# Seven half-block products for eight in the last transform chunks of layer two, fuller score steps, and an earlier gate for one layer norm

## The chip, the cores and the metric

One Trainium2 chip, one of its cores. The metric is the device time of one launch in microseconds; lower is better. The profile is one execution, recorded instruction by instruction.

## The reference

Two layers, each an attention block with a compressive memory and then a Fourier block, on 2048 rows of 512, with 32 heads of 16 in 4 segments of 512 rows:

```python
qs, ks, vs = q[:, :, s], k[:, :, s], v[:, :, s]
logits = einsum("bhqd,bhkd->bhqk", qs, ks) * scale + mask
a_dot = einsum("bhqk,bhkd->bhqd", softmax(logits), vs)
a_mem = einsum(phi(qs), M) / (einsum(phi(qs), z) + 1e-6)
o = g * a_mem + (1.0 - g) * a_dot
M, z = M + einsum(phi(ks), vs), z + phi(ks).sum
...
a = einsum("bsd,ed->bse", x, dft_hid_re)
b = einsum("bsd,ed->bse", x, dft_hid_im)
y = einsum("ts,bse->bte", dft_seq_re, a) - einsum("ts,bse->bte", dft_seq_im, b)
...
x = x + A(layernorm(x)); x = x + B(layernorm(x))
x = x + A(layernorm(x)); x = x + B(layernorm(x))
```

The second transform, along the sequence, is the largest product: 2048 x 2048 cosines on `a` and as many sines on `b`, in each layer.

## The kernel before

Products are made from pairs of half-precision numbers, a high and a low part, so that each takes three matmuls (`mm3`: high by high, high by low, low by high).

The program's order is not written by hand. Each part is a generator (`s_x`, `s_st`, `s_f` and so on) that yields what its next step needs: an engine, tiles to read, buffers to take, or a gate, a condition on what was done. The class `Plan` keeps a model of each engine's clock, of tiles and of buffers (52 of work in SBUF, 8 banks of PSUM), and the loop at the end of `body` always issues the step that could begin first by that model. So the instructions of an engine stand in a fixed order that follows from the planner's costs, and at run time each engine takes its own in that order. `ready` adds a reserve to some reads. All recorded instructions have the line of the helper that issues them (L249 before), so the profile names them by tiles: `w` is a work buffer, `b` a PSUM bank, `g` the transposed norm of a segment, `qst` and `kst` the queries and keys of a group, `vt` its values, `mx` the maxima of its scores, `mhl` their negatives in two halves, `y` the sum of the Fourier block (and at the start a place for raw weights), `cs` the raw table of cosines and sines, `cc` its prepared copy in DRAM, `fyu` the scale that a piece of it was divided by.

**Attention** goes by segment (`q`, 8 in two layers) and group of 8 heads (4 a segment; `i` counts all 32). `s_ln` loads a segment's four row tiles, `t_ln` norms them and writes them transposed into `xt`. It begins a segment `q` when the values of the last group of the segment before are projected, `gate(("V", q * NG - 1))`. `s_p` and `s_v` project. `s_x` makes the scores once for their row maxima (`t_max` on DVE), `s_st` makes them again transposed with the maxima folded in; `t_sel` takes the exponential on ACT and zeroes what lies above the diagonal on POOL; `s_av` multiplies by the values. A step of `s_x` or `s_st` fills two PSUM banks, one for each half of the heads (64 rows of the array each, side by side). For key tile `t` of four a score block is 128, 256, 384 or 512 columns wide, and a step holds as many blocks of one `t` as fit into 512: 11 steps a group, four of them with 384 columns.

**The Fourier block.** `s_ab` makes `a` and `b` of a row tile (the matmuls with `wd`), `t_ab` splits them into `ab`. `s_r` loads the raw tables once, `s_c` finds a scale for each batch of four pieces and splits and stores them. `s_f` then multiplies: a chunk is two row tiles, eight chunks a layer; for each of 16 output tiles `t` the unit (chunk `j`, `t`) is 12 matmuls of 512 columns (2 row tiles, 2 for `a` and `b`, 3 for the parts), which DVE scales and adds into `y`:

```python
for i, (x, z) in enumerate(((0, 0), (0, 1), (1, 0))):
    T.matmul(p, c[:, x, sl], b[:, z], start=(k == 0 and i == 0), stop=(k == 4 * n - 1 and i == 2))
...
spawn(t_y(p, layer, t, fyu[:, f:f + 1]), hots)
```

Layer two's units stand in the order of chunks; each output tile is stored after its eighth unit. Layer one keeps this form in the change too.

## Time and profile before

| | |
|---|---|
| median of 3 runs | 1781.19 us (1776.84 to 1781.40) |
| the profiled execution | 1784.39 us, span 1782.6 us |
| mean granted clock | 0.975 |
| matmuls, loads of weights | 11020 each |
| DMA | 242.43 MB, mean 136 GB/s |

The span runs from the first to the last instruction. A row of the profile gives a group of instructions: line, engine, operation, output and inputs, partitions x columns and type, count, then busy time in us and the mean length of one in ns, then the idle time of the engine just ahead of them and what ended it. The lengths of matmuls overlap, so what one takes in a stream is its group's busy time, or the distance of starts, divided by the count. PEld is the loading of weights, SPq the queue of SP, which issues all DMAs in order.

### The profile page before, as it was taken

The numbers are of one execution on the slowest core, as the hardware profiler recorded it, in microseconds if no ns is written. First come the engines' busy times: TensorE is split into PE (matmuls) and PEld (weight loads), VectorE is DVE, ScalarE is ACT, GpSimd is POOL, SyncE is SP. The second block draws the span as 40 slices with busy tenths as digits, with TensorE's granted clock in tenths as the row PEclk, the third lists the DMA queues.
The fourth block names the chain that finished last, engine by engine and source line by source line (L and its number), as shares of the span: only waits on it lengthen the run. The fifth ranks groups of instructions, "written<-read, shape, count | busy, mean of one in ns | idle before, by whom it ended". The sixth has DMA issues, their size and how long they took to land.

```text
span 1782.6 us, 32540 instructions
## 1 busy us (share of the span) xinstructions
PE 1676.7 (94%) x11020; PEld 733.9 (41%) x11020; DVE 1086.1 (61%) x3387; ACT 911.4 (51%) x1585; POOL 755.4 (42%) x1187
## 2 busy tenths in 40 slices
PE   4978799999999999999899998999999999999999
PEld 2424334344444433444444443444444443344444
DVE  7783777477667775545577656754676566342222
ACT  4567666756656758433456764556355535510000
POOL 6354545546544655433335543433553343330000
PEclk9978899999999999999899999999999999999999
DMA  8446536555555533435856745453453542137104
GB/s 214 118 129 155 163 106 142 174 154 154 150 134 158 164 90 116 133 123 171 237 160 195 206 138 131 100 138 110 118 126 107 164 99 71 51 107 254 42 0 136
DMA packets 240983, 242.43 MB, mean 136 GB/s; under 512 B 129776, under 2 KB 152304, under 8 KB 240816
## 3 DMA queue, kind: packets, MB, share of 16 engines
q1 hardware_dynamic: 240816, 240.35, 48.5%
q8 instruction: 87, 1.43, 0.4%
q14 instruction: 80, 0.66, 0.1%
HBM read 152.96 MB, written 63.70 MB: 122 GB/s over the span
## 4 chain that ended last, share of the span: by engine, by line
PE 67%; DMA 11%; DVE 7%; ACT 5%; POOL 4%; issue 4%; SPq 2%; POOLq 0%; ACTq 0%; DVEq 0%
PE b L249 67%; ACT w L249 5%; POOL w L249 3%; DMA w<-w 3%; DVE w L249 2%; SPq L249 2%; DVE junk L249 2%; DMA dc<-den 2%; DMA w<-rec 2%; DMA w<-in_cs_dram 1%; DVE cam L249 1%; DVE bst L249 1%; DMA w<-in_x_dram 1%; DVE y L249 0%; DMA d<-w 0%
## 5 line engine op out<-in xcount | busy, mean ns | idle before, releaser
L249 PE MATMUL b<-w,w 128*128 128x512 f16 x3072 | 714.1, 382 | 12.5 <-ACT w L249 7.1
L249 PEld LDWEIGHTS <-w 128*128 128x128 f16 x4992 | 465.4, 99 | 624.4 <-issue 111.2
L249 POOL TENSOR_TENSOR w<-w,w 128x512 f16<-128x512 f32 (+1 forms) x316 | 379.6, 1208 | 369.1 <-ACT w L249 255.3
L249 ACT ACTIVATE w<-b,fac 128x512 f32<-128x512 f32 (+1 forms) x728 | 420.0, 657 | 205.6 <-PE b L249 196.2
L249 DVE CUSTOM_DVE_ANT_0 junk<-b,cmask 128x128 bf16<-128x128 f32 (+3 forms) x1024 | 441.1, 484 | 105.3 <-PE b L249 104.2
L249 POOL TENSOR_SCALAR_AFFINE_SELECT w<-w 128x128 f32<-128x128 f32 (+2 forms) x704 | 242.8, 356 | 308.6 <-ACT w L249 285.2
L249 DVE SCALAR_TENSOR_TENSOR y<-b,fyu,y 128x512 f32<-128x512 f32 x232 | 173.3, 747 | 220.4 <-PE b L249 219.7
L249 ACT ACTIVATE w<-b 128x512 f16<-128x512 f32 (+1 forms) x240 | 137.9, 597 | 178.7 <-PE b L249 172.3
L249 ACT ACTIVATE w<-w,csc 128x512 f16<-128x512 f32 (+1 forms) x256 | 181.9, 723 | 70.2 <-DVE csc L249 53.6
L249 PE MATMUL b<-g,w 128*128 128x512 f16 x768 | 187.5, 386 | 3.6 <-DMA g<-w 2.8
L249 PE MATMUL b<-wd,w 128*128 128x512 f16 x768 | 181.4, 382 | 0.1
L249 ACT ACTIVATE w<-w 128x512 f16<-128x512 f32 (+1 forms) x144 | 90.5, 631 | 177.9 <-DVE w L249 122.1
L249 PE MATMUL b<-w,vt 128*32 128x512 f32 (+3 forms) x2048 | 177.7, 455 | 1.9 <-POOL w L249 1.7
L249 DVE SCALAR_TENSOR_TENSOR w<-b,w 128x512 f16<-128x512 f32 x128 | 87.8, 687 | 100.4 <-ACT w L249 100.0
L249 PE MATMUL b<-kst,qst 62*128 62x128 f16 (+3 forms) x1024 | 124.7, 305 | 18.1 <-ACT w L249 5.6
L249 PE MATMUL b<-qst,kst 64*128 64x512 f16 (+3 forms) x1024 | 121.1, 304 | 13.3 <-ACT w L249 7.7
L249 PE MATMUL b<-w,g 128*128 128x128 f16 x1536 | 97.4, 221 | 11.9 <-DMA w<-w 6.9
L249 PEld LDWEIGHTS <-g 128*128 128x128 f16 x1536 | 89.7, 99 | 26.9 <-issue 17.7
L249 PEld LDWEIGHTS b<-w,vt 128*32 128x32 f32 x2048 | 56.5, 111 | 96.4 <-issue 51.1
L249 PE MATMUL b<-wo,w 128*128 128x512 f16 x384 | 88.0, 385 | 0.9 <-ACT w L249 0.9
L249 PEld LDWEIGHTS <-kst 64*128 64x128 f16 x1024 | 37.5, 94 | 124.5 <-issue 118.8
L249 DVE TENSOR_REDUCE cam<-w 128x1 f32<-128x512 f32 x128 | 81.0, 675 | 6.8 <-DMA w<-in_cs_dram 6.7
(101 smaller groups left out, 902.8 us busy)
## 6 DMA issues: line engine op xcount, KB each, us to landing
w<-in_cs_dram SPq DMA_DIRECT2D x128, 256.0 KB
cc<-w SPq DMA_DIRECT2D x128, 256.0 KB
w<-cc SPq DMA_DIRECT2D x128, 256.0 KB
w<-w SPq DMA_DIRECT2D x96, 256.0 KB
d<-w SPq DMA_DIRECT2D x128, 128.0 KB
w<-rec SPq DMA_DIRECT2D x56, 256.0 KB
w<-in_x_dram SPq DMA_DIRECT2D x32, 256.0 KB
qst<-d SPq DMA_DIRECT2D x64, 128.0 KB
```

What stands on the lines that cost most here:

```text
L249: r = f(*args, **kw)
```

## The change

**Seven products for eight.** In layer two, chunks five to seven (`WIN` = 5) no longer go through units. For a chunk and a pair of output tiles `t`, `t+1` the tables form a block matrix of two by two (a block: 128 outputs by 256 of the chunk's inputs), and the chunk's `a`, `b` another one of two by two (halves of 256 columns). The product of the two, eight block products before, is made by seven products of sums and differences (`t_win`, six matmuls of 256 columns each, in three PSUM banks), which DVE adds into `y` in halves. Four blocks of the tables are combined ahead of time from the raw ones (`s_b`: DVE or POOL adds, ACT and DVE split, SP stores them as `sc`), from the end of layer two's first segment on. The combinations of `a` and `b` are made in `t_six`, after `t_full` has taken them from PSUM at full precision. The two tiles of a pair share one scale, so `s_c` takes the maximum over both. Per pair four tiles of tables are loaded for two before (`win`), the last as a half. The last chunk's output tiles are stored two at a time (`t_out`).

**Fuller score steps.** `steps` lets a step hold blocks of different `t`: in `s_x` those of 128 with those of 384 columns, in `s_st` the same for the second and fourth key tile. 10 steps a group, all of 512 columns. `s_av` takes the key tiles in the order 0, 2, 1, 3.

**The gate of segment two.** `s_ln` begins segment two (`q` = 1) when the first group's value products are done (`("E", 0)`), no longer when the last group's values are projected.

**The planner's reserve** in `ready` is 1500 ns (`AGAIN`) where the first entry of what is read's key is `"y"`; `key` gives a pair of the tile's full name and a row for tiles kept by rows, as `y` is.

```diff
+WIN = 5
...
+AGAIN = 1500.0
...
-            r = max(r, self.wr.get(n, 0.0) + (RESERVE.get(self.by.get(n), 0.0) if eng == "T" else 500.0 * (eng != "Y" and self.by.get(n) == "Y")))
+            r = max(r, self.wr.get(n, 0.0) + (AGAIN if n[0] == "y" else RESERVE.get(self.by.get(n), 0.0) if eng == "T" else 500.0 * (eng != "Y" and self.by.get(n) == "Y")))
...
-                yield gate(("V", q * NG - 1))
+                yield gate(("E", 0) if q == 1 else ("V", q * NG - 1))
...
+    def steps(widths, *groups):
+        out = []
+        for ts in groups:
+            per = 512 // sum(widths[t] for t in ts)
+            for p0 in range(0, NP, per):
+                o, step = 0, []
+                for p in range(p0, p0 + per):
+                    for t in ts:
+                        step.append((p, t, o, widths[t]))
+                        o += widths[t]
+                out.append(step)
+        return out
...
-            for t in range(TT):
-                n = 128 * (t + 1)
-                w = 512 // n
...
+            for step in steps([128 * (t + 1) for t in range(TT)], (1,), (0, 2), (3,)):
...
-        v3 = pt[:, :w * n].rearrange("k (w n) -> k w n", w=w)[:, :, 0:128]
+        w = len(step)
+        v3 = pt.rearrange("k (c n) -> k c n", n=128)[:, 0:4 if w > 1 else 1:step[-1][2] // 128 if w > 1 else 1, :]
...
+            for step in steps([512 - 128 * t for t in range(TT)], (0,), (2,), (1, 3)):
...
-            for t in range(TT):
+            for t in (0, 2, 1, 3):
...
+    def s_b():
+        yield gate(("cd", npiece - 1), ("O", 4))
+        pl.floor("bg", 3)
+        pl.floor("sp", 1)
+        lo, hi = slice(0, 256), slice(256, 512)
+        for j in range(WIN, nch):
+            for t in range(0, NT, 2):
+                c = csu[:, fyat[j, t]:fyat[j, t] + 1]
+                yield need("Y", tag=("bg", "bg", "bg"))
+                a, b, d = (sb("bg") for _ in range(3))
+                Y.dma_start(a, cs[j, t])
+                Y.dma_start(b, cs[j, t + 1])
+                yield need("VG", a, b)
+                tt(d[:, lo], b[:, lo], b[:, hi], OP.add)
+                yield need("VG", a, d)
+                tt(d[:, hi], d[:, lo], a[:, lo], OP.subtract)
+                yield need("VG", a, b)
+                tt(a[:, lo], a[:, lo], b[:, lo], OP.subtract)
+                pl.close(b)
+                yield need("VG", a, d)
+                tt(a[:, hi], a[:, hi], d[:, hi], OP.subtract)
+                for i, x in enumerate((d, a)):
+                    yield need("A", x, tag="sp")
+                    o = sb("sp", F16, (128, 2, 512))
+                    A.activation(o[:, 0], x, AF.Copy, scale=c)
+                    yield need("V", x, o)
+                    V.scalar_tensor_tensor(o[:, 1], x, c, o[:, 0], op0=OP.mult, op1=OP.subtract)
+                    pl.close(x)
+                    yield need("Y", o)
+                    Y.dma_start(sct[j, t + i], o)
+                    pl.close(o)
+                done.add(("sd", j, t))
...
+    def t_six(gt, e):
+        yield gate(("full", gt, e), ("full", gt + 1, e))
+        a, b = fulls.pop((gt, e)), fulls.pop((gt + 1, e))
+        lo, hi = slice(0, 256), slice(256, 512)
+        out = []
+        yield need("VG", a, b, tag=("sd", "sd"))
+        c, d = sb("sd"), sb("sd")
+        tt(c[:, lo], a[:, hi], a[:, lo], OP.subtract)
+        yield need("VG", b, c)
+        tt(c[:, hi], b[:, hi], c[:, lo], OP.subtract)
+        yield need("VG", a, b)
+        tt(d[:, lo], b[:, hi], a[:, hi], OP.subtract)
+        yield need("VG", b, c)
+        tt(d[:, hi], b[:, lo], c[:, hi], OP.subtract)
+        for x in (a, b, c, d):
+            w = 256 if x is a else 512
+            yield need("A", x, tag="wb")
+            o = sb("wb", F16, (128, 2, w))
+            A.activation(o[:, 0], x[:, :w], AF.Copy)
+            yield need("VG", x, o)
+            tt(o[:, 1], x[:, :w], o[:, 0], OP.subtract)
+            pl.close(x)
+            out.append(o)
+        sixes[gt, e] = out
+        done.add(("six", gt, e))
...
+                if layer and j >= WIN:
+                    continue
...
+                yield need("T", c0, s0, *[b[0] for b in bs], tag=("dft", "dft", "dft"))
+                banks = [ps("dft") for _ in range(3)]
+                spawn(t_win(j, t, f, bs, (c0, s0, s1, c1), banks), hots)
+                if j == nch - 1:
+                    spawn(t_out(t, ("add", j, t)), hots)
+            spawn(t_done(j, bs))
+    def t_win(j, t, f, bs, tiles, banks):
+        def mul(o, c, at, i, off, first, last):
+            for e in range(2):
+                for n, (x, z) in enumerate(((0, 0), (0, 1), (1, 0))):
+                    T.matmul(o, c[:, x, at + 128 * e:at + 128 * e + 128], bs[e][i][:, z, off:off + 256],
+                             start=first and e == 0 and n == 0, stop=last and e == 1 and n == 2,
+                             skip_group_check=True)
+        def add(p, src, dst, key, *more):
+            yield need("V", p)
+            V.scalar_tensor_tensor(dst, src, f, dst, op0=OP.mult, op1=OP.add)
+            pl.close(*more)
+            done.add(key)
+        k = "add", j, t
+        c0, s0, s1, c1 = tiles
+        px, py, pz = banks
+        yield need("T", c0, s0, *[b[0] for b in bs])
+        mul(px[:, :256], c0, 0, 0, 0, True, True)
+        spawn(add(px, px[:, :256], y[:, t, :256], (*k, 0)), hots)
+        yield need("T", s0, *[b[2] for b in bs])
+        mul(py[:, :256], s0, 0, 2, 0, True, True)
+        spawn(add(py, py[:, :256], y[:, t + 1, 256:], (*k, 1)), hots)
+        yield need("T", c0, *[b[1] for b in bs])
+        mul(pz[:, :256], c0, 256, 1, 0, True, True)
+        pl.close(c0)
+        yield gate((*k, 0))
+        yield need("T", s0, y[:, t, :256], *[b[2] for b in bs])
+        mul(px[:, :256], s0, 256, 2, 256, False, True)
+        pl.close(s0)
+        spawn(add(px, px[:, :256], y[:, t, 256:], (*k, 2)), hots)
+        yield need("T", c1, *[b[3] for b in bs])
+        mul(pz[:, 256:], c1, 0, 3, 256, True, True)
+        pl.close(c1)
+        spawn(add(pz, pz.rearrange("p (a n) -> p a n", a=2), y[:, t:t + 2, 0:256], (*k, 3), pz), hots)
+        yield gate((*k, 1))
+        yield need("T", s1, y[:, t + 1, 256:], *[b[1] for b in bs])
+        mul(py[:, :256], s1, 256, 1, 256, False, True)
+        spawn(add(py, py[:, :256], y[:, t, 256:], (*k, 4), py), hots)
+        yield gate((*k, 2))
+        yield need("T", s1, y[:, t, 256:], *[b[3] for b in bs])
+        mul(px[:, :256], s1, 0, 3, 0, False, True)
+        pl.close(s1)
+        spawn(add(px, px[:, :256].unsqueeze(1).to_broadcast([128, 2, 256]),
+                  y[:, t + 1, :].rearrange("p (a n) -> p a n", a=2), (*k, 5), px), hots)
+        done.add(("wf", j, t))
...
+    def t_out(t, k):
+        yield gate(*[(*k, i) for i in range(6)])
+        for i in range(2):
+            yield need("Y", y)
+            Y.dma_start(fins[1][t + i], y[:, t + i, :])
```

How the order of instructions moves is seen at three places.

SP's queue where the loads of segment two's input (`w<-in_x_dram`) and of the weights `wo` and `wd` are issued; `g1` is the segment's transposed norm, `den`, `dc` and `rec` the division by the softmax sums of an earlier group, `mhl` the maxima. Before:

```order
L249 DMA y_84<-in_wo_dram 128x4x512
L249 DMA y_84<-in_wd_dram 128x4x1024
L249 DMA dc_1355<-den_1318 128x32
L249 DMA w14_1375<-in_x_dram 128x512
L249 DMA rec_1319<-dc_1355 128x32
L249 DMA w39_1563<-in_x_dram 128x512
L249 DMA w42_1582<-rec_1319 128x1x512
L249 DMA_TRANSPOSE g1_1468<-w45_1616 128x8x128
L249 DMA den_1674<-w43_1666 4x512
L249 DMA den_1674<-w46_1668 4x512
L249 DMA dc_1680<-den_1674 128x32
L249 DMA w48_1687<-in_x_dram 128x512
```

And now:

```order
L251 DMA w10_1317<-in_x_dram 128x512
L251 DMA w17_1327<-in_x_dram 128x512
L251 DMA w14_1357<-in_x_dram 128x512
L251 DMA den_1388<-w16_1332 4x512
L251 DMA den_1388<-w13_1334 4x512
L251 DMA dc_1408<-den_1388 128x32
L251 DMA w21_1415<-in_x_dram 128x512
L251 DMA_TRANSPOSE g1_1321<-w19_1392 128x8x128
L251 DMA qst1_108<-mhl_1331 1x16x128 x4
L251 DMA y_84<-in_wo_dram 128x4x512
L251 DMA y_84<-in_wd_dram 128x4x1024
```

Three of the four loads stand ahead of the division and of `wo` and `wd`, the fourth and the first transpose ahead of the maxima of group one (`qst1<-mhl`); before, the loads followed `wd` one by one.

PE in the scores for the maxima of group one, between projections (`g0`) of the last group of segment one; `b` numbers are banks. Before, for the third row tile:

```order
L249 LDWEIGHTS w30_813
L249 MATMUL b6_995<-g0_280,w30_813 128x512
L249 LDWEIGHTS qst1_108
L249 MATMUL b0_1010<-kst1_105,qst1_108 128x384
L249 LDWEIGHTS qst1_108
L249 MATMUL b4_1011<-kst1_105,qst1_108 128x384
L249 LDWEIGHTS w30_813
L249 MATMUL b6_995<-g0_280,w30_813 128x512
```

And now, the first and third row tile together:

```order
L251 LDWEIGHTS w29_771
L251 MATMUL b4_999<-g0_328,w29_771 128x512
L251 LDWEIGHTS qst1_108
L251 MATMUL b3_1036<-kst1_105,qst1_108 128x128
L251 LDWEIGHTS qst1_108
L251 MATMUL b0_1037<-kst1_105,qst1_108 128x128
L251 LDWEIGHTS qst1_108
L251 MATMUL b3_1036<-kst1_105,qst1_108 128x384
L251 LDWEIGHTS qst1_108
L251 MATMUL b0_1037<-kst1_105,qst1_108 128x384
L251 LDWEIGHTS w29_771
L251 MATMUL b4_999<-g0_328,w29_771 128x512
```

The step of two score matmuls of 384 columns between projections has become one of four that fills both banks.

DVE at the end of the program, the additions into `y` from PSUM banks. Before, one for each unit:

```order
L249 SCALAR_TENSOR_TENSOR y_84<-b3_22148,fyu_275,y_84 128x512
L249 SCALAR_TENSOR_TENSOR y_84<-b0_22163,fyu_275,y_84 128x512
L249 SCALAR_TENSOR_TENSOR y_84<-b7_22178,fyu_275,y_84 128x512
L249 SCALAR_TENSOR_TENSOR y_84<-b6_22193,fyu_275,y_84 128x512
L249 SCALAR_TENSOR_TENSOR y_84<-b4_22208,fyu_275,y_84 128x512
```

And now, six for each pair of tiles:

```order
L251 SCALAR_TENSOR_TENSOR y_84<-b4_23023,fyu_275,y_84 128x256
L251 SCALAR_TENSOR_TENSOR y_84<-b6_23024,fyu_275,y_84 128x256
L251 SCALAR_TENSOR_TENSOR y_84<-b0_22962,fyu_275,y_84 128x512
L251 SCALAR_TENSOR_TENSOR y_84<-b4_23023,fyu_275,y_84 128x256
L251 SCALAR_TENSOR_TENSOR y_84<-b5_23025,fyu_275,y_84 128x2x256
L251 SCALAR_TENSOR_TENSOR y_84<-b6_23024,fyu_275,y_84 128x256
L251 SCALAR_TENSOR_TENSOR y_84<-b4_23023,fyu_275,y_84 128x512
```

Additions of half width and double ones stand in place of one full addition per output tile; `b4` appears three times, since PE goes on accumulating in that bank after DVE has read it.

149 lines of the change are left out of this document (101 added, 48 removed).

## The prediction

> **What bounds the kernel now.** I read the page's busy shares first, then the chain that ended last, then the busy time by stage. Of the chain 67% is TensorE.
>
> ```profile
> span 1782.6 us, 32540 instructions
> PE 1676.7 (94%) x11020; PEld 733.9 (41%) x11020; DVE 1086.1 (61%) x3387; ACT 911.4 (51%) x1585; POOL 755.4 (42%) x1187
> ...
> PE 67%; DMA 11%; DVE 7%; ACT 5%; POOL 4%; issue 4%; SPq 2%; POOLq 0%; ACTq 0%; DVEq 0%
> ```
>
> The stages differ. Columns: length, then busy time of PE, PEld, DVE, ACT, POOL, then granted clock, DMA share, GB/s.
>
> ```profile
> 50.00:250.00 200.00, 168.85 (x1220) 72.25 (x1218) 141.19 (x522) 127.28 (x226) 95.40 (x165) 0.87 0.52 135
> 250.00:1540.00 1290.00, 1243.31 (x8459) 539.19 (x8457) 830.26 (x2624) 743.34 (x1293) 606.53 (x954) 0.99 0.51 139
> 1540.00:1783.00 243.00, 238.86 (x1163) 107.16 (x1162) 74.94 (x110) 18.16 (x32) 22.09 (x30) 1.00 0.32 104
> ```
>
> From 50 to 250 us PE idles 31 us and runs at a clock of 0.87. Until 1540 it idles 47 us of 1290 (3.6%), and then it is full to the end, its 4 idle us lying behind the last matmul. So work taken from PE late is worth its whole time; work given to it early is worth the idle it fills, as long as the other engines keep up, and the busiest of them, DVE, has 61%.
>
> **The tail.** Chunks five to seven of layer two are the last 576 matmuls, in one run:
>
> ```profile
> 1654.38 124.48 PE L249 MATMUL b<-w,w 128*128 128x512 f16 x576
> L249 PE MATMUL b<-w,g 128*128 128x128 f16 x1536 | 97.4, 221 | 11.9 <-DMA w<-w 6.9 <-ACT w L249 3.0 <-POOL w L249 1.7
> ```
>
> 124.48/576 = 216.1 ns for 512 columns, 213.3 of them streaming at the 2.4 columns a nanosecond that fits both rows. The change does the 24 row-tile pairs in 7 products of 6 matmuls of 256 columns: 1008, streaming 106.7 ns each. No row has this shape. Its overhead lies between 2.8 ns (as at 512 columns) and 10.1 ns (97.4/1536 = 63.4 at 128 columns, 53.3 streaming): 110.4 to 117.7 us. I take 111.5 ns, nearer the first since the second row also holds early matmuls at a low clock: 112.4 us, **-12** (-14 to -7). By the Trainium skill, "TensorE: Matmul & The Clock Gate", section "Back-to-back issue gap", a matmul of N columns costs N/2.4 + 2.5 ns, which would be 110 us; the same section says that a stream with weight loads takes about 81 ns at 128 columns, and this trace's 63.4 is against that.
>
> Between the products DVE must add a half block before PE may accumulate in that bank again; two products lie between.
>
> ```profile
> 1778.90 0.75 DVE L249 SCALAR_TENSOR_TENSOR y<-b,fyu,y 128x512 f32<-128x512 f32 x1 [1.84 <-PE b L249]
> L249 PE MATMUL b<-cam,ones 128*128 128x4 f32 x64 | 10.6, 236 | 3.3 <-DVE cam L249 2.8 <-ACT w L249 0.3
> ```
>
> A 512-wide add takes 0.75 us, so a half one at most that, and two products take 1.3 us: it is covered, by 0.5 us. DVE has per pair four half adds and two full ones, 4.5 us at the very most against PE's 4.7. Behind the last matmul one full add and two stores in place of one: **+1**. The scales of these chunks take 12 more ones-matmuls (44 for 32), at 10.6/32 = 0.33 us at most: **+3** (+2 to +4).
>
> **Fewer, fuller score steps.** A group's scores now need 10 steps twice for 11 twice, 640 for 704. What counts is PE's change between full-array matmuls, half-array scores and quarter-array products:
>
> ```profile
> 248.44 0.39 PE L249 MATMUL b<-qst,kst 64*128 64x512 f16 x2
> 248.77 1.47 PE L249 MATMUL b<-w,w 128*128 128x512 f16 x6
> 250.17 0.61 PE L249 MATMUL b<-qst,kst 64*128 64x512 f16 x4
> 250.71 1.47 PE L249 MATMUL b<-w,w 128*128 128x512 f16 x6
> ```
>
> Start to start, six matmuls take 1.40 us where 6 x 216.1 ns are 1.30, and two scores take 0.33 and four 0.54, so 0.21 for two and 0.12 for the run itself: 0.11 us a run. In the order PE has 908 such runs before and 805 after, and most of the difference, 84, is there with the fuller steps alone. 103 x 0.11 = **-11** (0 if they fall into idle time, -15 if quarter-array runs cost more). The exponentials are eight of 384 columns fewer and six full ones more per group:
>
> ```profile
> L249 ACT ACTIVATE w<-b,fac 128x512 f32<-128x512 f32 x472 | 290.8, 694 | 137.3 <-PE b L249 128.3 <-issue 7.0 <-POOL w L249 1.0
> L249 ACT ACTIVATE w<-b,fac 128x384 f32<-128x384 f32 x256 | 130.7, 587 | 68.3 <-PE b L249 67.9
> ```
>
> 32 x (6 x 0.616 - 8 x 0.511), by busy time, is -12 us of ACT, and DVE's maxima are the same. Neither bounds PE after 250 us, so I count nothing.
>
> **Segment two's layer norm.** Its input loads stand before, in the queue of SP, around and behind the loads of wo and wd, which are 3 MB:
>
> ```profile
> 89.92 0.59 SPq L249 DMA_DIRECT2D y<-in_wo_dram  x1
> 90.56 0.50 SPq L249 DMA_DIRECT2D y<-in_wd_dram  x1
> ...
> 91.64 0.65 SPq L249 DMA_DIRECT2D w<-in_x_dram  x1
> 101.81 0.33 SPq L249 DMA_DIRECT2D rec<-dc  x1
> 102.19 0.43 SPq L249 DMA_DIRECT2D w<-in_x_dram  x1
> ...
> 119.58 0.40 SPq L249 DMA_DIRECT2D w<-in_x_dram  x1
> 127.39 5.74 SPq L249 DMA_TRANSPOSE g<-w  x2
> ```
>
> So its projections start at 137 us, and until then PE runs dry:
>
> ```profile
> 110.00:120.00 10.00, 4.94 (x24) 1.71 (x25) 9.93 (x50) 3.35 (x7) 2.00 (x3) 0.55 0.30 66
> 120.00:130.00 10.00, 8.61 (x41) 1.73 (x39) 9.63 (x28) 9.19 (x19) 7.99 (x18) 0.60 0.32 80
> ...
> 113.19 0.40 PE L249 MATMUL b<-identf,mx 128*32 128x128 f32 x1 [4.56 <-DVE mx L249]
> ...
> 137.21 1.04 PE L249 MATMUL b<-g,w 128*128 128x512 f16 x4 [0.58 <-DMA w<-w]
> ```
>
> From 113 to 137 us, 24 us, PE does what at full clock would take about 9 (2.4 columns a nanosecond, scores two and values four side by side): 15 lost. In the new order the loads go ahead, and the projections stand right around the second transpose of maxima, the instruction that waits here at 113.19. Their last transpose still queues behind wo and wd (10 us, 91.64 to 101.81 above), so I put their start near 111 to 118 us. The price: DVE does three norms, and SP a transpose, ahead of group one's maxima, which its scores wait for. Statistics and scaling of one:
>
> ```profile
> L249 DVE BATCH_NORM_STATS2 bst<-w 128x6 f32<-128x512 f32 x56 | 38.5, 688 | 8.9 <-DMA w<-in_x_dram 4.6 <-DMA w<-x 3.8
> L249 DVE TENSOR_SCALAR w<-w,mv,rs 128x512 f32<-128x512 f32 x56 | 39.0, 696 | 14.4 <-POOL rs L249 14.2
> ```
>
> Three make 4 us, and I put as much again on the first load's landing and the transpose: up to 8 us in which PE has little else. 15 less 8 is 7; a part of the wait at 113 stays, so **-6** (-15 to +5). DVE is full from 110 to 130 (9.93 and 9.63 of 10), so it, not the projections, may stay the bound there.
>
> **The combined tables.** For 24 pairs: two raw loads, four half-block additions, two splits, two stores, before the last groups of layer two are done. By the nearest rows:
>
> ```profile
> L249 POOL TENSOR_TENSOR macc<-macc,w 128x256 f32<-128x256 f32 x16 | 11.8, 735 | 15.2 <-DVE w L249 12.5 <-DVE dc L249 2.6
> L249 ACT ACTIVATE w<-w,csc 128x512 f16<-128x512 f32 x128 | 92.6, 724 | 66.1 <-DVE csc L249 53.6 <-POOL rs L249 10.4 <-issue 2.1
> L249 DVE SCALAR_TENSOR_TENSOR w<-w,w 128x512 f16<-128x512 f32 x32 | 26.3, 822 | 32.0 <-ACT w L249 32.0
> ...
> 250.00:800.00 550.00, 532.29 (x3549) 0.99 0.50 139
> 1049.00:1560.00 511.00, 499.89 (x3558) 0.99 0.43 112
> ```
>
> 24 x (4 x 0.735 + 2 x 0.724 + 2 x 0.822) = 145 us on three engines, none of it on PE, over about 500 us. The last two rows (PE's busy time, clock, DMA) give the price of such a load: with the first preparation of the tables, 128 pieces of about 3.3 us, PE idles 3.2%; without it 2.2%. A third of that load over 511 us is 2 us, and the combinations of the chunks' own halves, hidden by the AB matmuls and the previous chunk, 1: **+3** (0 to +10). DMA in the tail rises to 896 KB per pair of 4.7 us, about 200 GB/s, and 310 with the stores of the last chunk. Before, PE stayed full in the fourth slice from the end, which moved 254:
>
> ```profile
> PE   4978799999999999999899998999999999999999
> ...
> GB/s 214 118 129 155 163 106 142 174 154 154 150 134 158 164 90 116 133 123 171 237 160 195 206 138 131 100 138 110 118 126 107 164 99 71 51 107 254 42 0 136
> ```
>
> The planner's 1500 ns never apply: the key of a row of y begins with the tile's full name, y_84 in the order's rows, not with "y", so that part of the change does nothing, and the instructions stand the same without it. The new order of the value products acts only through the runs counted above.
>
> **Sum.** -12 + 1 + 3 - 11 - 6 + 3 = -22. The profiled execution took 1784.4 us, 1.8 more than its span, and is 3.2 above the median shown; -22 gives 1762.4 for it and **1759** at the median. About 0.3%, 5.3 us, is what a measurement of this kernel can tell from no change.
>
> **Rivals.** (1) The early gain doesn't come: the norms ahead of group one's maxima cost what the projections fill, since DVE is the full engine there. The term is +2: 1767, chance 0.15. (2) The half products have the overhead of the 128-column row, or DVE's adds come 0.1 us late at the three joints of each pair (72 x 0.1): 5 to 7 us less gain, 1765, chance 0.10. (3) Slower: the preparation between 1080 and 1560 us blocks queues that work in order. ACT or POOL stands at a combination whose load or partner is late, and the exponentials and masks behind it, which free the score banks, stand too; PE then waits once per pair. It turns the sign at 25/24 = 1.0 us per pair (the other terms give -25), and at 1.5 gives 1792. For it, the waits from 1080 to 1560 us (total, times, longest) already have POOL behind ACT:
>
> ```profile
> POOL w L249 <- ACT w L249: 189.4, 177, 11.1
> ...
> L249 PEld LDWEIGHTS <-w 128*128 128x128 f16 x4992 | 465.4, 99 | 624.4 <-issue 111.2 <-ACT w L249 9.9 <-POOL w L249 5.2
> ```
>
> Against it: the first preparation, three times this load, costs PE 1%. Chance 0.06. (4) Weight loads don't hide under half-width matmuls: 432 more loads of 99 ns (the last row above), all exposed, make 1759 + 43 = 1802. The 128-column row, 63 ns per pair of load and matmul, is against it. The Trainium skill, same page, section "The mechanism", lets a load overlap a running matmul only where the row group differs; by that rule this rival would hold, and the trace disagrees with its 63 ns. Chance 0.02. That the change doesn't do what it says is ruled out by the order, which has the 1008 half matmuls and the moved loads.
>
> **Numbers.** Forecast 0.67, rivals 0.15, 0.10, 0.06, 0.02. With every term at its better end the sum is -41 (1740), with every term at its worse +13 (1794), which takes six independent misses. The range, 1740 to 1779, holds the first, rivals 1 and 2, and the forecast with up to 20 us of misses; rivals 3 and 4 and the rest, some 0.15, are left out. Faster by over 0.3% (below 1775.8): 0.86; within: 0.07; slower: 0.07.
>
> **What would show it.** Right: PE's last run of 1008 matmuls in 111 to 114 us without idle gaps; projections of segment two before 120 us, and PE's busy time from 110 to 130 near 18; PE's idle from 1049 to 1560 below 15 us; start-to-start distances as above with fewer runs. Wrong: a DVE wait ahead of the half matmuls, PE idle from 85 to 105 us longer than the 15 us lost later, or waits for ACT and POOL after 1080 that add up to over 10 us.

## The result, and the profile after

| | kernel before | changed kernel |
|---|---|---|
| median, first comparison | 1781.4 us (9 runs) | 1772.56 us (9 runs) |
| ratio, 95% interval | | 0.9941 [0.9924, 0.9959], that is -10.5 us (-13.5 to -7.3) |
| same comparison once more | 1781.55 us (13 runs) | 1772.97 us (8 runs), 0.9942 [0.9922, 0.9963] |
| profiled execution | 1784.4 us, span 1782.6 | 1774.87 us, span 1772.8 |

The forecast was 1759, a gain of 22; the gain is 10. Times below are against the median of before, as (ratio - 1) x 1781 us.

The page of the changed kernel, to be read beside that of before: its busy times, and the chain that ended last.

```profile
span 1772.8 us, 33983 instructions
...
PE 1665.3 (94%) x11476; PEld 791.9 (45%) x11476; DVE 1170.4 (66%) x3538; ACT 942.8 (53%) x1593; POOL 848.2 (48%) x1248
...
PE 63%; DVE 10%; DMA 10%; ACT 6%; issue 5%; POOL 4%; SPq 2%; POOLq 0%; ACTq 0%; DVEq 0%
```

PE is busy 11.4 us less (1676.7 before), and its idle time, span less busy time, grew from 105.9 to 107.5 us. The three other engines work 31 to 93 us more. By stage, first the three of the prediction, then the early windows, then two long stretches (columns: length, PE busy, PEld, DVE, ACT, POOL, granted clock, DMA share, GB/s):

```profile
50.00:250.00 200.00, 172.59 (x1243) 75.85 (x1242) 144.89 (x549) 128.23 (x221) 96.18 (x163) 0.86 0.51 133
250.00:1540.00 1290.00, 1238.53 (x8448) 550.30 (x8447) 867.74 (x2658) 752.61 (x1268) 653.78 (x964) 0.99 0.57 158
1540.00:1773.00 233.00, 227.93 (x1611) 150.25 (x1608) 118.49 (x206) 39.76 (x70) 66.88 (x84) 1.00 0.48 152
...
85.00:110.00 25.00, 20.17 (x152) 8.40 (x153) 23.34 (x84) 16.34 (x29) 14.13 (x27) 0.80 0.75 195
110.00:130.00 20.00, 17.58 (x150) 8.65 (x150) 15.29 (x58) 11.19 (x22) 5.86 (x11) 1.00 0.62 165
250.00:800.00 550.00, 533.29 (x3547) 236.74 (x3546) 364.98 (x1078) 341.43 (x572) 280.58 (x399) 0.99 0.51 142
1049.00:1560.00 511.00, 488.60 (x3448) 209.62 (x3443) 341.66 (x1070) 282.23 (x487) 269.40 (x434) 1.00 0.57 159
```

Three things are to be seen. From 110 to 130 us PE gained 4 us (13.55 before). From 250 to 800 us nothing changed (532.29 before). And from 1049 to 1560 us, where the combined tables are prepared, PE idles 511 - 488.6 = 22.4 us where it idled 511 - 499.89 = 11.1; DMA went from 112 to 159 GB/s there.

The tail, TensorE's timeline (start, length, tiles, shape, count, and in brackets the idle time ahead with its releaser):

```profile
1649.97 36.84 PE L251 MATMUL b<-w,w 128*128 128x256 f16 x336
1686.65 7.93 PE L251 MATMUL b<-wd,w 128*128 128x512 f16 x36
1694.42 57.82 PE L251 MATMUL b<-w,w 128*128 128x256 f16 x528
1753.18 15.89 PE L251 MATMUL b<-w,w 128*128 128x256 f16 x144 [0.95 <-DMA w<-cc]
```

336 half matmuls take 1686.65 - 1649.97 = 36.68 us, 109.2 ns each; all 1008 take 36.68 + 58.76 + 15.89 = 111.3 us with the one wait of 0.95 in them, 13.1 less than the 124.5 of before. The adds between the products are on time (VectorE's timeline near the end): each waits for PE, none is waited for.

```profile
1759.94 0.48 DVE L251 SCALAR_TENSOR_TENSOR y<-b,fyu,y 128x256 f32<-128x256 f32 x1 [0.17 <-PE b L251]
1760.60 0.48 DVE L251 SCALAR_TENSOR_TENSOR y<-b,fyu,y 128x256 f32<-128x256 f32 x1 [0.17 <-PE b L251]
1761.25 0.75 DVE L251 SCALAR_TENSOR_TENSOR y<-b,fyu,y 128x512 f32<-128x512 f32 x1 [0.17 <-PE b L251]
...
1769.11 0.75 DVE L251 SCALAR_TENSOR_TENSOR y<-b,fyu,y 128x512 f32<-128x512 f32 x1 [0.17 <-PE b L251]
```

Segment two's projections, which began at 137 us, now begin at 112.3, around the transpose of maxima that PE waited for. And a change of mode costs what it did: six full matmuls take 1433.82 - 1432.42 = 1.40 us from start to start, the two scores behind them 0.32.

```profile
112.34 0.82 PE L251 MATMUL b<-g,w 128*128 128x512 f16 x3
113.89 0.28 PE L251 MATMUL b<-identf,mx 128*32 128x128 f32 x1 [0.73 <-DVE mx L251]
114.02 2.10 PE L251 MATMUL b<-g,w 128*128 128x512 f16 x9
...
1432.42 1.47 PE L251 MATMUL b<-w,w 128*128 128x512 f16 x6
1433.82 0.39 PE L251 MATMUL b<-qst,kst 64*128 64x512 f16 x2
1434.14 2.76 PE L251 MATMUL b<-wo,w 128*128 128x512 f16 x12
```

So the tail, the norm's early effect and the price of a mode change came out as forecast, and the 12 us are missing elsewhere. The trace names one place (1049 to 1560 us) and leaves open what became of the runs saved. Theory A: the combined tables cost some 13 us, not 3. Theory B: fewer runs save nothing, because they lie where PE waits anyway. Theory C: the same for the early norm.

### The profile page after: what moved, and what is told of

Its sections match the earlier page's. It is cut to its first block, busy times and chain, and to the rows that moved or that the text cites. A ratio compares the mean times of both kernels' runs of the same rounds, so it can differ in the third digit from the quotient of the medians.

```text
span 1772.8 us, 33983 instructions
## 1 busy us (share of the span) xinstructions
PE 1665.3 (94%) x11476; PEld 791.9 (45%) x11476; DVE 1170.4 (66%) x3538; ACT 942.8 (53%) x1593; POOL 848.2 (48%) x1248
## 4 chain that ended last, share of the span: by engine, by line
PE 63%; DVE 10%; DMA 10%; ACT 6%; issue 5%; POOL 4%; SPq 2%; POOLq 0%; ACTq 0%; DVEq 0%
PE b L251 63%; ACT w L251 5%; POOL w L251 4%; DVE junk L251 3%; DVE w L251 3%; SPq L251 2%; DMA w<-w 2%; DMA w<-rec 1%; DMA dc<-den 1%; DMA w<-in_cs_dram 1%; DMA den<-w 1%; DMA w<-x 1%; DVE y L251 1%; DMA w<-cc 1%; DVE bst L251 1%
## 5 line engine op out<-in xcount | busy, mean ns | idle before, releaser
L251 PE MATMUL b<-w,w 128*128 128x512 f16 (+1 forms) x3504 | 692.1, 349 | 8.9 <-POOL w L251 3.8
L251 POOL TENSOR_TENSOR w<-w,w 128x512 f16<-128x512 f32 (+3 forms) x417 | 463.6, 1119 | 454.0 <-ACT w L251 318.8
L251 ACT ACTIVATE w<-b,fac 128x512 f32<-128x512 f32 x664 | 406.8, 695 | 132.2 <-PE b L251 129.7
L251 DVE CUSTOM_DVE_ANT_0 junk<-b,cmask 128x256 bf16<-128x256 f32 (+3 forms) x1024 | 436.5, 483 | 46.7 <-PE b L251 46.2
L251 POOL TENSOR_SCALAR_AFFINE_SELECT w<-w 128x256 f32<-128x256 f32 (+1 forms) x640 | 232.7, 378 | 216.8 <-ACT w L251 211.4
L251 DVE SCALAR_TENSOR_TENSOR y<-b,fyu,y 128x512 f32<-128x512 f32 (+1 forms) x328 | 216.4, 668 | 134.7 <-PE b L251 134.3
L251 ACT ACTIVATE w<-w,csu 128x512 f16<-128x512 f32 (+1 forms) x304 | 216.2, 722 | 108.2 <-DVE csu L251 65.1
L251 ACT ACTIVATE w<-b 128x512 f32<-128x512 f32 (+1 forms) x240 | 137.1, 597 | 233.7 <-PE b L251 230.5
L251 ACT ACTIVATE w<-w 128x512 f16<-128x512 f32 (+2 forms) x168 | 103.4, 622 | 168.3 <-DVE w L251 116.7
L251 PE MATMUL b<-kst,qst 62*128 62x256 f16 (+3 forms) x1024 | 123.0, 308 | 23.7 <-DVE mx L251 10.3
L251 PE MATMUL b<-qst,kst 64*128 64x512 f16 (+3 forms) x1024 | 123.1, 308 | 16.4 <-ACT w L251 7.0
```

What stands on the lines that cost most here:

```text
L251: r = f(*args, **kw)
```

## Experiments, first set: one part at a time

**Fuller score steps alone.** Before, with the steps, the masks and the order of the value products of the change:

```diff
-            for t in range(TT):
-                n = 128 * (t + 1)
-                w = 512 // n
+            for step in steps([128 * (t + 1) for t in range(TT)], (1,), (0, 2), (3,)):
...
```

> The kernel before with the fuller score steps alone (84 fewer runs of PE's order, 824 for 908). If 0.11 us a run is really saved (theory A: the missing gain went to the combined tables), about -9 us against before. If the distance between runs is only idle time that other waits fill again (theory B), between -3 and +1 us.

Measured: 1792.22 us (12 runs), ratio 1.0044 [1.0024, 1.0064], **+8 us**. Neither theory said that.

**Early layer norm alone.**

```diff
-                yield gate(("V", q * NG - 1))
+                yield gate(("E", 0) if q == 1 else ("V", q * NG - 1))
```

> The kernel before with segment two's layer norm freed earlier, alone. By the forecast's term -6 us, in theories A and B alike. If the early gain is given back because what it fills is waited for again by 320 us (theory C, from the stretch-by-stretch difference of the two traces), between -2 and +2 us.

Measured: 1789.71 us (12 runs), 1.0037 [1.0017, 1.0057], **+7 us**. Outside all three theories as well.

**Seven products alone.** The changed kernel with the score steps and the gate of before:

```diff
-                yield gate(("E", 0) if q == 1 else ("V", q * NG - 1))
+                yield gate(("V", q * NG - 1))
...
-            for step in steps([512 - 128 * t for t in range(TT)], (0,), (2,), (1, 3)):
+            for t in range(TT):
+                n = 512 - 128 * t
+                w = 512 // n
...
```

> The kernel before with the seven products alone, with all that prepares them. PE's last run gives -13 by the trace. Theory A (the combined tables cost some 13 us beside the other work, not 3): +2 to +6 us in all. Theories B and C (they cost about 3): -5 to -8 us.

Measured: 1798.82 us (6 runs), 1.0080 [1.0056, 1.0105], **+14 us**, though its tail is as fast as that of the changed kernel. Theory A's sign, and more than its size.

**The change without the preparation of its tables.**

```diff
-                for i, (d, n) in enumerate(((cct[place[j, t]], 0), (sct[j, t], 0), (sct[j, t + 1], 0),
+                for i, (d, n) in enumerate(((cct[place[j, t]], 0), (cct[place[j, t]], 0), (cct[place[j, t + 1]], 0),
...
-                Y.dma_start(a, cs[j, t])
-                Y.dma_start(b, cs[j, t + 1])
...
-                    Y.dma_start(sct[j, t + i], o)
...
```

> The changed kernel without the preparation of the combined tables: for each of the 24 pairs the two raw loads, four half-block additions, two splits and two stores are left out, and the two combined pieces are loaded from the plain tables instead, so that PE does the same products on wrong data. Theory A: 10 to 15 us faster than the changed kernel, so about -20 to -24 against before. Theories B and C: 2 to 4 us faster than the changed kernel, about -12 to -14 against before.

Measured: 1762.38 us (6 runs), 0.9876 [0.9846, 0.9906], **-22 us**: 11.6 faster than the changed kernel, as theory A has it, with some 6 us of play either way from the two intervals. By the medians the tables carry most of the miss; but the parts, +8, +7 and +14 one at a time, don't add up to -10. That needed a cause of its own.

## Second set: what in the tables costs the time

The changed kernel again as the yardstick, then its preparation with the DMAs alone, with the arithmetic alone, and begun late.

> The changed kernel unchanged, as the yardstick for the three kernels beside it: -9 to -12 us against before.

Measured: 1772.97 us, 0.9942 [0.9922, 0.9963], -10 us, as before.

```diff
-                yield need("VG", a, b)
-                tt(d[:, lo], b[:, lo], b[:, hi], OP.add)
...
-                    A.activation(o[:, 0], x, AF.Copy, scale=c)
...
+                for i, x in enumerate((b, a)):
+                    yield need("Y", x)
+                    Y.dma_start(sct[j, t + i], x)
+                    pl.close(x)
```

> The changed kernel in which the preparation of the combined tables keeps its DMAs (two raw loads and two stores of 256 KB per pair, at the same place) and leaves out the additions, scalings and splits; the stored pieces are not used, the products read the plain tables. If the 12 us that the preparation costs come from engines that work in order (theory A1): no more than 3 us slower than without the preparation, about -18 to -22 us against before. If they come from its DMA traffic (theory A2): as slow as the changed kernel.

Measured: 1770.43 us (6 runs), 0.9925 [0.9899, 0.9951], -13 us: by the medians 9 of the 12 us are there with the DMAs alone.

```diff
-                Y.dma_start(a, cs[j, t])
-                Y.dma_start(b, cs[j, t + 1])
+                if (j, t) == (WIN, 0):
+                    Y.dma_start(a, cs[j, t])
+                    Y.dma_start(b, cs[j, t + 1])
...
-                    Y.dma_start(sct[j, t + i], o)
```

> The changed kernel in which the preparation keeps its additions, scalings and splits on ACT, POOL and DVE, but loads its raw pair once instead of 24 times and stores nothing; the products read the plain tables. Theory A1 (engines in order): as slow as the changed kernel, about -9 us against before. Theory A2 (DMA traffic): -18 to -22 us.

Measured: 1763.15 us (6 runs), 0.9888 [0.9862, 0.9913], -20 us: the arithmetic alone costs 2 of the 12. That speaks for A2, the traffic, and against A1, engines that work in order, but the intervals of these two kernels overlap a little. The window from 1130 to 1520 us shows more, one row each of before, of the kernel without the preparation, of the changed kernel, of that with the DMAs alone and of that with the sums alone:

```profile
1130.00:1520.00 390.00, 384.38 (x2768) 164.46 (x2767) 242.80 (x825) 209.52 (x378) 168.26 (x302) 1.00 0.46 118
```
```profile
1130.00:1520.00 390.00, 380.89 (x2704) 165.85 (x2697) 244.06 (x822) 200.13 (x350) 157.57 (x266) 0.99 0.45 114
```
```profile
1130.00:1520.00 390.00, 374.07 (x2655) 163.95 (x2647) 264.24 (x841) 216.06 (x373) 209.96 (x326) 1.00 0.62 168
```
```profile
1130.00:1520.00 390.00, 372.26 (x2634) 163.98 (x2633) 231.00 (x786) 192.20 (x334) 151.29 (x255) 0.99 0.60 161
```
```profile
1130.00:1520.00 390.00, 379.80 (x2676) 165.14 (x2674) 274.62 (x846) 221.53 (x384) 221.76 (x338) 1.00 0.44 115
```

PE idles 5.6, 9.1, 15.9, 17.7 and 10.2 us. The DMAs alone, with DVE, ACT and POOL busy even less than before, cost as much PE time as the whole preparation; the sums alone, with all three busier than in any other row, 1.1 us more than no preparation. Over all kernels of this study the window splits the same way: eight traces with the traffic (161 to 169 GB/s) have PE idle 14.4 to 17.7 us, twelve without it (112 to 118 GB/s) 5.6 to 13.0; the means are 15.7 and 9.1.

A window fixed in time holds different work in different orders. From PE's transpose of the twentieth group's maxima to that of the thirty-second, the last, PE idles 16.3 us without the preparation, 18.0 with the sums alone, 24.9 with the DMAs alone and 24.0 in the changed kernel. These four kernels reach the first of the two points at 1021 to 1025 us, and from the fourth group's transpose to it their PE does the same number of matmuls, within two. So no difference of order ahead of the preparation parts them. Over all traces the means of that stretch are 22.8 us with the traffic and 15.8 without, but not without overlap (one with it has 16.7, one without it 21.5).

The engines' own instructions don't get longer by the traffic. ACT's exponentials in that window take 695 ns without the tables and 694 with the DMAs alone; VectorE's longest maxima, in the same two kernels (count, busy, mean ns):

```profile
L251 DVE CUSTOM_DVE_ANT_0 junk<-b,cmask 128x512 bf16<-128x512 f32 x80 | 51.3, 683 | 6.7 <-PE b L251 6.6
```
```profile
L251 DVE CUSTOM_DVE_ANT_0 junk<-b,cmask 128x512 bf16<-128x512 f32 x64 | 40.5, 682 | 7.0 <-PE b L251 7.0
```

The waits of PE from 1049 to 1560 us, before and in the changed kernel (releaser, total us, times, longest), show no one place where it is lost; it waits longer for maxima, for ACT and for POOL, and hardly differently for the DMAs themselves:

```profile
PE b L249 <- DMA w<-w: 4.1, 2, 2.9
PE b L249 <- DVE mx L249: 2.2, 6, 1.1
PE b L249 <- ACT w L249: 0.9, 4, 0.4
PE b L249 <- POOL w L249: 0.8, 1, 0.8
```

```profile
PE b L251 <- DVE mx L251: 7.3, 13, 1.6
PE b L251 <- ACT w L251: 4.6, 12, 1.4
PE b L251 <- DMA w<-w: 3.5, 3, 1.7
PE b L251 <- POOL w L251: 2.8, 3, 1.8
```

Is it the traffic itself, or that SP, which takes its DMAs in order, stands at them with the score path's transfers behind? SP's wait for VectorE's split is its longest in the changed kernel from 1130 to 1520 us, run again; so the first kernel of the next set issues the same DMAs later.

**Tables begun late.**

```diff
-        yield gate(("cd", npiece - 1), ("O", 4))
+        yield gate(("cd", npiece - 1), ("X", NGRP - 1))
```

> The changed kernel with the preparation of the combined tables begun when the last group's maxima are done (about 1540 us) instead of after layer two's first segment (about 1080 us); nothing left out. From there to the first of the seven products are 110 us in which ACT and POOL are under 40% busy and PE only streams. If the preparation costs what it takes from the score path (theory A1 or A2): 9 to 12 us faster than the changed kernel, about -20 against before. If the tables come late for the products (24 pairs in the time from 1540 us, 9 us each, are too slow): PE waits for the combined pieces after 1650 us and it is no faster than the changed kernel, by 1 us per pair up to +24.

Measured: 1820.87 us (6 runs), 1.0216 [1.0187, 1.0245], **+39 us**. The second expectation, and worse. Its tail by windows, and PE's waits from 1540 us:

```profile
1600.00:1650.00 50.00, 48.10 (x262) 25.35 (x261) 25.81 (x42) 8.45 (x12) 18.54 (x23) 1.00 0.62 199
1650.00:1700.00 50.00, 43.00 (x344) 32.90 (x342) 35.12 (x59) 11.78 (x20) 22.69 (x24) 1.00 0.63 215
1700.00:1750.00 50.00, 37.73 (x314) 31.05 (x312) 33.08 (x59) 9.62 (x16) 19.52 (x23) 0.94 0.71 243
1750.00:1820.00 70.00, 44.34 (x326) 34.64 (x325) 33.53 (x59) 7.22 (x10) 14.73 (x19) 0.87 0.62 216
```
```profile
PE b L251 <- DMA w<-cc: 35.9, 14, 6.1
PE b L251 <- POOL w L251: 5.0, 2, 3.9
```

PE waits 36 us for table pieces while ACT is under 24% busy and POOL under 46%; the loads of these pieces are late. Why isn't settled: the mean rate is 215 to 243 GB/s, but SP, which also issues these loads in its order, stands 74 us at VectorE's splits from 1640 us on. The rate alone is no limit here, since the changed kernel moves 271 GB/s from 1753 to 1769 us with PE busy 15.8 us of 16. The Trainium skill, "DMA: Bandwidth & Descriptors", section "Specifications", puts a core's limit at about 358 GB/s of HBM traffic. The means of these windows lie well below it, so the limit of the total is no test of whether a transfer is in time.

## Third set: SP's queue, and the other corners

```diff
+        yield lambda: pl.free["T"] >= at + 4000.0
+        yield need("Y", o)
+        Y.dma_start(sct[j, t + i], o)
...
+                yield lambda: pl.free["T"] >= till + 4000.0
                 yield need("Y", tag=("bg", "bg", "bg"))
...
-                    yield need("Y", o)
-                    Y.dma_start(sct[j, t + i], o)
+                    spawn(t_store(j, t, i, o, pl.last(o.tensor.name)))
```

> The changed kernel with the DMAs of the preparation issued later in SP's order: the two stores of a pair 4 us (planned) after the split that they store, the next pair's raw loads 4 us after the last split; one more 256 KB buffer for the pieces, the same bytes over the same stretch. If the preparation costs PE's time because SP, which takes its DMAs in order, stands at the stores until VectorE's split is done (SP's waits for that are 55 us from 1130 to 1520 us in the changed kernel, 11 without the preparation; theory A3): those fall below 20 us and the time to about -17 against before. If the traffic itself delays the other transfers (theory A2): as the changed kernel, -8 to -12.

Measured: 1778.16 us (12 runs), 0.9989 [0.9970, 1.0008], -2 us: no gain, and 8 us slower than the changed kernel, which neither expectation has. SP's waits from 1130 to 1520 us, of the changed kernel, run again, and of this one:

```profile
SPq L251 <- DVE w L251: 54.8, 28, 9.8
SPq L251 <- ACT w L251: 20.8, 23, 4.3
```
```profile
SPq L251 <- ACT w L251: 35.6, 16, 10.2
SPq L251 <- DVE w L251: 32.7, 16, 8.2
```

The stand at VectorE's splits fell by 22 us only, not below 20, that at ACT rose by 15, and PE's idle time in the window stayed (15.1 to 14.4 us, 168 GB/s). In the kernel with the DMAs alone SP stands at VectorE for 16.5 us, near the 11.0 without the preparation, and PE idles most; but there SP stands another 24.3 us at raw loads that it stores again. That speaks against SP's stand as the cause; since much of it remained in each, it isn't excluded.

Then three kernels that take one part out. The edits are those of the first set, reversed: the old score steps in the changed kernel, the old gate in it, and before with steps and gate but without the seven products.

> The changed kernel with the score steps of before, 901 runs of PE's order for 805. By the forecast's term of 0.11 us a run on the path: 11 us slower than the changed kernel, about +1 against before. If the runs saved lie in stretches where PE waits anyway and the term is nothing: -8 to -12. If the parts added up as they did one at a time (+7 and +14): about +20.

> The changed kernel with segment two's layer norm at its old place. By the forecast's term: 6 us slower than the changed kernel, about -4 against before. If the early gain is given back before 600 us: -8 to -12. If the parts added up as they did one at a time (+8 and +14): about +20.

> The kernel before with the fuller steps and the early layer norm, without the seven products. By the forecast's terms (96 runs fewer and the norm): -17. If both fall into idle time: -3 to +3. If the parts added up as they did one at a time (+8 and +7): about +15.

Measured: 1788.05 us, 1.0045 [1.0028, 1.0061], +8; 1784.86 us, 1.0022 [1.0008, 1.0036], +4; and 1766.46 us (6 runs), 0.9925 [0.9908, 0.9943], **-13**, the best so far of the kernels that leave nothing out. The first two meet none of their three expectations; the third is nearest to the forecast's terms, -17, which lie just outside its interval (-16.4 to -10.2). All eight corners, in us against before:

| | without the seven products | with them |
|---|---|---|
| old steps, old norm | 0 | +14 |
| fuller steps | +8 | +4 |
| early norm | +7 | +8 |
| fuller steps and early norm | -13 | -10 |

The steps' effect is +8, -20, -10 and -18 us by what stands beside them (mean -10), the norm's +7, -21, -6 and -14 (mean -9), the seven products' +14, -4, +1 and +3 (mean +4). No reading of an edit ("nothing", "its term", "additive") holds in every corner.

## Fourth set: why the corners scatter

In the traces so far PE waits from 835 to 875 us for pieces that ACT and POOL make, 2.5 to 9.1 us in all. Theory D: the first preparation sets when layer one ends, and swallows what PE saved earlier.

```diff
                 A.activation(cc[:, 0], raw, AF.Copy, scale=sc)
-                A.activation(raw, raw, AF.Copy, scale=sc)
```

> The kernel before with one of the two ScalarE passes over each of the 128 raw table pieces left out (the scaling in place, 0.72 us each; the split then subtracts from the unscaled piece, so the tables are wrong). If the preparation of the tables sets the time at which layer one's last products end, at 860 to 870 us, whatever PE saved earlier (theory D): that point comes 10 us or more earlier and the time falls by 10 to 20 us. If not: -3 to +5.

> The same with the fuller score steps. Theory D: what the steps save before 870 us now shows, and it is 6 to 12 us faster than the lighter preparation alone. If fuller steps by themselves make the kernel slower, or save nothing (theory B): as slow as the lighter preparation alone, or up to 10 us slower, as without it.

Measured: 1792.33 us (8 runs), 1.0048 [1.0030, 1.0066], **+9** with 92 us of ScalarE's work left out; and 1770.18 us, 0.9924 [0.9904, 0.9945], -14 with the steps, 22 less than without. The second has theory D's sign, and more than its 6 to 12; the first is against it. No wait for ACT or POOL is left in its trace from 835 to 925 us, and it is slower with less work. Theory E took its place: each edit makes the planner deal out the whole order anew, and an order moves the time by itself. So two kernels with no edit but a number of the planner:

```diff
-HOLD, SWITCH = 700.0, 95.0
+HOLD, SWITCH = 700.0, 96.0
```

> The kernel before with one number of the planner changed, the price of a change of PE's mode, 96 ns for 95; the same work and the same instructions, dealt out in another order from the second group on (902 runs for 908). If an order dealt anew moves the time by itself (theory E: the reason why the fuller steps alone, the norm alone and the lighter preparation alone came out 7 to 8 us slower), 5 to 12 us away from before, to either side. If order alone matters little: -3 to +3 us, and each of those three has a cause of its own.

```diff
-TWICE, EARLY, BESIDE = 1000.0, 0.0, 1000.0
+TWICE, EARLY, BESIDE = 1010.0, 0.0, 1000.0
```

> The changed kernel with one number of the planner changed, the price of a score step that takes the second pair of banks, 1010 ns for 1000; the same work in another order from the third group on (808 runs for 805). Theory E: 5 to 12 us away from the changed kernel, to either side, so -22 to -15 or -5 to +2 against before. If order alone matters little: -7 to -13.

Measured: 1792.55 us, 1.0064 [1.0048, 1.0080], **+11** from the same work; and 1776.20 us (12 runs), 0.9969 [0.9951, 0.9988], -6, 5 slower than the changed kernel. For before, theory E is shown: the interval, 8 to 14 us, is far from 0. For the changed kernel it is weaker: the 5 us are barely more than the two intervals leave open, and -6 lies between the two expectations. Two rows of the kernel dealt anew from before (its profiled execution, 1798.2 us, is 6 above its median):

```profile
250.00:1540.00 1290.00, 1237.27 (x8346) 537.57 (x8345) 820.14 (x2602) 729.21 (x1263) 593.02 (x927) 0.99 0.51 139
1540.00:1797.00 257.00, 252.70 (x1287) 110.69 (x1285) 86.52 (x145) 35.53 (x64) 32.16 (x57) 1.00 0.31 98
```

From 250 to 1540 us it had PE busy 6.0 us less than before (1243.31), by idle time, and did that work at the end. That is half of the 13.8 us by which its span is longer. The other half is PE itself: over the whole execution it is busy 1683.5 us, 6.8 more than before, with the same 11020 matmuls, and the trace doesn't say why. If the order of before is one of the better ones, as one other order of the same work suggests, +8, +7 and +9 for single edits are no verdict on them.

Last, fewer chunks in the new way, with their tables begun at 1510 us:

```diff
-WIN = 5
+WIN = 7
...
-        yield gate(("cd", npiece - 1), ("O", 4))
+        yield gate(("cd", npiece - 1), ("X", NGRP - 1))
```

> The changed kernel with the seven products for the last chunk alone, its 8 pairs of tables prepared after the last maxima (1510 us on), 190 us before PE needs them; nothing left out. Without traffic beside the score path it should keep the fuller steps' and the norm's -13, and gain the third of the tail's 13, less 1 at the end and 1 for scales: -15 to -17 against before. If the transfers in the tail hold PE up as they did with 24 pairs: -5 or more.

> The same with the last two chunks, 16 pairs prepared from 1510 us, 150 us before PE needs the first. If the transfers keep up (16 MB of preparation, 110 GB/s on top of the 100 that the tail loads): -18 to -20 against before. If they don't: PE waits for the combined pieces by up to 1 us per pair, -5 to +5.

Measured: 1770.17 us (6 runs), 0.9919 [0.9895, 0.9943], -14; and (WIN = 6) 1773.34 us (6 runs), 0.9932 [0.9906, 0.9959], -12, between its two expectations. PE's waits from 1510 us on, for one chunk and for two:

```profile
PE b L251 <- DMA w<-cc: 1.8, 4, 0.8
PE b L251 <- DMA w<-w: 0.7, 1, 0.7
```
```profile
PE b L251 <- DMA w<-cc: 4.1, 5, 1.2
PE b L251 <- DMA w<-w: 3.8, 3, 1.8
PE b L251 <- DVE y L251: 1.7, 1, 1.7
PE b L251 <- DMA w<-sc: 0.7, 1, 0.7
```

2.5 us of waits with 8 pairs, 10.3 with 16, over 40 with 24: they grow with the transfers in the tail. SP's stand at what VectorE writes, the splits among it, grows too (45, 109 and 122 us, the last from 1540 us on), so the amount of the transfers and their order aren't told apart. One chunk comes out as it should, within the interval; it, and the steps and norm without any, come out ahead of the changed kernel by 3 to 4 us, which their intervals don't part from it.

## Why the prediction was off, step by step

**The tail, -12 (-14 to -7).** Right: -13.1. A half matmul takes 109.2 ns (111.5 taken), weight loads hidden, adds on time, so rivals 2 and 4 are out. The Trainium skill's N/2.4 + 2.5 ns, given there for an isolated matmul ("TensorE: Matmul & The Clock Gate", section "Back-to-back issue gap"), is 109.2 ns for 256 columns. The trace agrees, in a stream.

**End of the program, +1.** Nothing: from PE's last matmul (1769.07) to the end are 3.7 us, as before.

**Twelve more ones-matmuls, +3.** As busy time right: their row went from 10.6 us (64 matmuls, two to each) to 13.5 us (88). The idle time ahead of them grew too, from 3.3 to 5.9 us, which the term leaves out. Tail, end and scales were forecast as -8 together; without the tables' preparation the seven products gain 22.1 - 13.4 = 8.7 over the kernel with steps and norm alone.

**The combined tables, +3 (0 to +10).** This is the step that failed. They cost about 12 us (11.6 by leaving them out, some 6 either way by the two intervals), just beyond the upper bound. Leaving them out also deals the order anew from about 1100 us on, so the firmer figure is PE's idle time from the twentieth to the last transpose of maxima: 24.0 us for 16.3 in kernels that are alike up to there, 24.9 with the DMAs alone, and 7 us more in the mean of all traces with the traffic. The sign named for it in the prediction, PE's idle time from 1049 to 1560 us below 15 us, was missed (22.4). I priced them as "a third of the load" of the first preparation, by how much PE idles in a stretch with it and in one without. Those two stretches differ in more than the preparation, and no run leaves the first preparation out, so that 1% was no price. Counting bytes would have given a third as well (24 MB for 64); what the term left out is what 24 MB of loads and stores do beside the score path's own transfers. Rival 3 named the place and a sign (slower by 1.0 us per pair to turn it), but its mechanism, ACT or POOL standing at a combination, isn't needed: the DMAs alone, with no combination in the kernel, cost 9 us, and the sums alone, whose loads can't be late, 2. PE's waits for ACT and POOL after 1080 us add up to 6.3 us, below the 10 that the prediction names as a sign, and 12/24 = 0.5 us per pair is below its turning point. Through which transfers the traffic reaches PE, and how much SP's order adds, stays open.

**Fewer runs, -11 (0 to -15), and the norm, -6 (-15 to +5).** Together -17 forecast, -13 (-16 to -10) measured without the seven products: the size is about right, 4 us too much. The price of a run is confirmed (1.40 and 0.32 us from start to start, as before), but by the order 66 of the 103 runs saved stand ahead of the maxima of the sixteenth group, at some 680 us, where PE has idle time to lose. The early gain came where it was put: projections from 112.3 us (111 to 118 forecast), PE busy 17.58 of 20 us from 110 to 130, and from 85 to 110 it idles 4.8 us, against 4.5 before, so the price of 8 us doesn't show as idle time. But in those 25 us PE did 152 matmuls for 185, at a granted clock of 0.80 for 0.93, so part of it may have been paid there. The changed kernel reaches the twentieth transpose of maxima 10.9 us ahead of before, about what 66 runs at 0.11 us, the norm and the scales add up to (-10, an estimate); but the one dealt anew from it is only 3.2 us ahead there, so the agreement is in part luck. Apart, the two terms can't be measured: their effects change by 28 us with what stands beside them.

**The sum.** -22 of forecast became -10: 8 us of the miss are the seven products with their tables (+3 for -5), 4 the steps and the norm. What the sum left out is the deal itself. It took the order as given and added terms, while 5 and 11 us came from one number of the planner; the 4 us that the steps and the norm lack are within that scatter and have no cause shown. The range, 1740 to 1779, held the time; the order's own scatter belongs in it by name.

## What to carry to other kernels

Where a planner or scheduler deals out the order, price an edit by the stretch that it works in, and first change a number that does no work, to learn what an order alone is worth: here 5 to 11 us, as much as the parts; a part's worth shows only in several settings. Extra DMA traffic beside a path of short dependent transfers cost the engine that waits at its end some 7 us here, though the instructions of VectorE and ACT got no longer and the DMA engines' busy share was 0.62. Work saved late, in a stream that is full, came out to the microsecond; work saved early, among waits, partly.

## What the hardware showed that I had not expected

A 24 MB stream of loads and stores beside the score path, 168 GB/s for 118, took 7 us of PE's time in 390, and the same arithmetic without it about 1. In a tail that needs 896 KB every 4.6 us, with the preparation beside it, PE waited 36 us for table pieces at mean rates of 215 to 243 GB/s; whether the rate or SP's order made them late stays open. The same work in another order kept PE busy 6.8 us longer. The same kernel's runs spread by some 16 us in several orders (1783.7 to 1799.9 for the steps alone), so that a profiled execution can lie 7 us from its median.
